# Loads, rounding steps and clamps moved in the start of a linear-attention and feed-forward kernel, and its last store split

## The chip, the cores and the metric

The kernel runs on one core of a Trainium2 chip. A core has a matrix engine (TensorE, PE in the profile, with its weight loads as PEld), a vector engine (VectorE, DVE), an engine for functions and copies (ScalarE, ACT), a general one (GpSimd, POOL) and a sequencer that issues transfers (SyncE, SP). Each takes its instructions in program order and waits on semaphores where an operand is not ready. TensorE writes to PSUM, the other engines compute between PSUM and the on-chip memory SBUF. The metric is the device time of one execution in microseconds (us); the lower the better.

## The reference, cut to what matters

```
# attention: B=4, H=8, S=768, D=48; q, k, v ~ 0.1 N(0,1), f_logit ~ 0.5 N(0,1) + 2
f = 1 / (1 + exp(-f_logit))
for t in range(S):
    state = f[:, :, t, :, None] * state + einsum('bhd,bhe->bhde', k[:, :, t], v[:, :, t])
    y[:, :, t] = einsum('bhd,bhde->bhe', q[:, :, t], state)
x = y as (3072 tokens, 384)
# feed-forward: w_in (384, 2048), w_out (2048, 384), both given as float64
h  = x @ w_in
sp = max(h, 0) + log1p(exp(-|h|))
out = (h * erf(sp)) @ w_out                     # (3072, 384), float32
```

## The kernel before, in words

The 3072 tokens are 24 chunks of 128 (six to a batch entry), taken as 12 blocks of two chunks. The recurrence is done chunk by chunk, and within a chunk in two halves of 64 tokens. Four functions make up a chunk g:

- `stage_d` (d): one prefix matmul of the block's log decays (L380) into PSUM, two Exp on ScalarE (L383, L386), eight small copies of the decay totals issued by SP (L391, from chunk 3 on), and on VectorE the products qd and kd (L395, L399).
- `stage_t` (t): eight transposes on TensorE (L411), copied out by ScalarE (L418 for q, L420 for k; k on VectorE, L422, from chunk 9 on). It also issues the second state update of the chunk before.
- `stage_s` (s): the outer products k v (L460) and the scores (L468) into one PSUM tile. For the first three chunks and from chunk 10 on VectorE masks the scores (L496); between these ScalarE copies them (L488) and GpSimd masks (L491). Then the first state update: four VectorE instructions, L438 and L439 twice.
- `stage_y` (y): 64 small matmuls (L525) that give the chunk's output, copied by ScalarE (L529) to `xT`, the input of the feed-forward part.

PSUM tiles of the tag "at" (prefix sums, both transposes, y) come from a ring of two, so y(g) waits for the copy L418 of the transposes issued two tiles ahead of it. The score tile has one buffer.

`prepare` makes the log decays of a block or of one chunk: a clamp on VectorE (L360), then Exp and Ln on ScalarE (L364, L365), with a load of the function table ahead (L347) when another was in use.

The feed-forward part of a block has four groups. A group is 12 slots of the main loop: `hidden` does four tiles of 128 hidden units with three matmuls each (a slot is one such matmul and appears as two L587 records), then ScalarE copies the group out (L594). `activate` does the nonlinearity of a group in a fixed train of calls to `act_step`: Exp (L157), two tanh (L160), two VectorE products (L165), three empty calls, one tanh (L559), one VectorE product (L561). A new group begins at the sixth call. Its Exp writes a buffer that the group two before has to free with L561. Groups of 1024 columns leave `hidden` through two PSUM tiles, so a group can begin only when the group two before has been copied out.

The weights arrive as float64 and are rounded to float32 on the chip. `load_piece` brings a piece of 768 KB into a spare place (SP, L292); `round_piece` rounds it in seven instructions: ScalarE's L311, then on VectorE L313, L317, L322, L326, L331 and L336. `weights_step` issues them one VectorE instruction at a time, six calls a piece; the call that issues L331 also issues L311 of the next piece. There are eight pieces of `w_in` and eight of `w_out`. A tile of the hidden layer may be issued only when its `w_in` piece is rounded (two tiles, six slots, to a piece), and the output matmuls need the `w_out` pieces.

The order of all instructions is written out by hand. A preamble does the first chunks (d(0), t(0), d(1), s(0), t(1), d(2), y(0), s(1), t(2), y(1)) with `weights_steps(2)` or `(4)` between them. Then the main loop makes twelve passes, `it` = 0 to 11. Pass 0 has 96 slots: the groups of blocks 0 and 1 in the order 0.0, 0.1, 1.0, 0.2, 1.1, 0.3, 1.2, 1.3. Pass 1 has the 48 slots of block 2. Pass 2 has the 48 slots of block 3 and then 32 of `project_first`, the output matmuls of block 0 (L670). Later passes do the output of one block by seven products in place of eight (`project`, L718) and the hidden layer of another; the last pass does the output of three blocks. After each slot the loop body, in this order, adds to `due` and issues one rounding step for each whole unit, issues a stage when the slot's number is next in the list `at`, issues clamp, Exp and Ln of a later block at fixed slots, and calls `act_step` at slots set by the pass (every sixth in pass 1, two in five in pass 2). So a rounding step in the program stands ahead of the stage and the activation step of the same slot on VectorE's queue.

In `project` the sums of the seven products are made on VectorE (L726) as they become complete, and `store` sends a block's 384 KB with one transfer on SP (L654).

Of the kernel before, what the change touches and what calls it, by code (L numbers as in the profile page):

```python
# [43 lines left out]
FP32 = mybir.dt.float32  # L44
# [26 lines left out]
P = 128  # L71
# [3 lines left out]
def kernel(  # L75
# [10 lines left out]
    nc = tc.nc  # L86
# [10 lines left out]
    CPB = 2  # L97
    TB = CPB * P
    n_blocks = B * S // TB
# [95 lines left out]
    DH = d_model // 2  # L195
# [147 lines left out]
    def use_exp_ln():  # L343
        if sets[0] == EXP_LN:
            return
        sets[0] = EXP_LN
        nc.scalar.add_instruction(  # L347
            mybir.InstLoadActFuncSet(
                act_func_set_id=EXP_LN, name=nc.get_next_instruction_name(),
                engine=mybir.EngineType.Activation, ins=[], outs=[],  # L350
            )
        )
# [3 lines left out]

    def prepare(blk, j0, j1):

        lt = lts[blk][:, j0:j1, :].rearrange("t j c -> t (j c)")
        nc.vector.tensor_scalar(  # L360
            out=lt, in0=lt, scalar1=LOGIT_MIN, scalar2=None, op0=ALU.max
        )
        use_exp_ln()
        nc.scalar.activation(out=lt, in_=lt, func=AF.Exp, scale=-1.0)  # L364
        nc.scalar.activation(out=lt, in_=lt, func=AF.Ln, bias=1.0)  # L365

    busy = []
# [284 lines left out]
    def store(blk):  # L652
# [4 lines left out]
        )  # L657

    def project_first(blk):

# [26 lines left out]
    def project(blk):  # L687
# [7 lines left out]
        }.items()}  # L695
        first = [1, 2, 5, 3]

        def pair(n):
# [38 lines left out]
        def fives():  # L737

            plus(o[:, 3:5, :], o[:, 4:5, :].broadcast_to((P, 2, DH)), pair(5))

        yield from products((2, 3), (5, 7))
        if end:

            fives()
        yield from products((2, 3), (3, 4))
        if not end:
            fives()
        plus(o[:, 1:3, :], o[:, 3:5, :], pair(3))
# [44 lines left out]
    with tc.manual_schedule():  # L793
# [7 lines left out]
        load_f(1)  # L801
        load(1, "qk")
        load_f(2)
        load_piece(0)
        load(1, "v")
        load(2)
        load_piece(1)
        load_piece(2)
# [47 lines left out]
        def weights_steps(n):  # L856
            for _ in range(n):
                weights_step()
# [6 lines left out]
        prepare(0, 1, 2)  # L865
        stage_t(0)
        load(3, "qk")
        load_piece(3)
# [44 lines left out]
        for it in range(n_blocks):  # L913
            gen, n = slots(it)
            if it == 0:
                todo = [(stage_s, 2), (stage_y, 2), (stage_d, 3), (stage_t, 3), (stage_s, 3), (stage_y, 3),
                        (stage_d, 4), (stage_t, 4), (stage_d, 5), (stage_s, 4), (stage_t, 5),
                        (stage_y, 4)] + stages(2)[4:]
                at = [1, 5, 6, 12, 16, 23, 34, 42, 48, 52, 60, 74, 76, 80, 88, 94]
            else:  # L920
                todo = stages(it + 2) if it + 2 < n_blocks else []
                at = [n * x // 48 for x in (2, 6, 11, 17, 25, 29, 34, 41)] if it == 1 else [int(3 + (n - 13) / max(1, len(todo)) * i) for i in range(len(todo))]
# [7 lines left out]
            for s, _ in enumerate(gen):  # L930
                due += (1 if s < 42 else 0.6 if s < 72 else 0.3) if it == 0 else 0.42 if it == 1 else 0.6
                while due >= 1:
# [4 lines left out]
                if at and s == at[0]:  # L937
# [3 lines left out]
                    if f in (stage_y, stage_y_s):  # L941
# [3 lines left out]
                        if g == 2:  # L945
                            load(5, "v")
                            load_piece(7)
                if it == 0 and s == 14:
                    prepare(2, 0, CPB)
                if it == 0 and s == 9:  # L950
                    load_f(6)
                    load_f(7)
                if s == n // 2 and it + 4 < n_blocks:
                    for j in range(CPB):
                        load_f((it + 4) * CPB + j)
                if it + 3 < n_blocks and s == prepare_at:
                    prepare(it + 3, 0, CPB)
                if it < 2:
# [242 lines left out]
```

## Time and profile before

| what | value |
| --- | --- |
| time, median of 7 runs | 618.9 us (618.78 to 619.81) |
| profiled execution | 619.97 us, its span 618.3 us |
| TensorE busy | 588.6 us (95%) |
| VectorE busy | 460.4 us (74%) |
| ScalarE busy | 382.3 us (62%) |
| pass 0 begins (first L587) | 28.33 us |
| pass 1, pass 2 begin | 105.92 us, 135.24 us |
| first output matmul (L670) | 164.4 us |
| last matmul ends | 611.1 us |

The span runs from the first to the last instruction; the time of an execution includes a little around it. "Busy" is the union of an engine's instructions. In a timeline row the first number is the start in us, the second the duration, then engine, line of the kernel, operation, what it writes and reads, shapes and count; what stands in brackets at its end is how long the engine stood idle before it and what ended the wait. The row PEclk gives the granted clock of TensorE in 40 equal slices, in tenths of full speed.

### The profile page before, as it was taken

What the parts mean: (1) busy time and instruction counts of PE and PEld (TensorE: products, weight loads), DVE (VectorE), ACT (ScalarE), POOL (GpSimd) and SP (SyncE); (2) the same over time, 40 slices, a digit from 0 to 9 for tenths busy, and PEclk for the clock granted to TensorE, in tenths of its full rate; (3) what the DMA queues carried; (4) which work ended last, traced back from release to release, by engine and by line L of the source; (5) the groups of instructions that cost most, each with busy time, mean ns of one, the idle gap of its engine ahead of it and who ended that gap; (6) DMA issues with size and microseconds to landing.
All of it is one profiled execution on the core that took longest, in us unless ns stands there. A gap on an engine that the chain in (4) does not pass through costs nothing.

```text
span 618.3 us, 13765 instructions
## 1 busy us (share of the span) xinstructions
PE 588.6 (95%) x5729; PEld 514.5 (83%) x5729; DVE 460.4 (74%) x784; ACT 382.3 (62%) x483; POOL 15.2 (2%) x33
## 2 busy tenths in 40 slices
PE   8778899999999999999999999999999999999995
PEld 7556687888655689989989989989989989989995
DVE  4998998697499597897796776896886785647451
ACT  5735357987875778775866675875766566366000
POOL 1000011010000000000000000000000000000000
PEclk9987899999999999999999999999999999999999
DMA  9996753350241223223223222132121000000000
GB/s 206 252 259 180 201 157 63 65 103 10 50 77 27 51 54 52 43 62 54 44 60 53 45 59 53 29 77 53 34 46 14 3 27 0 28 1 0 27 27 29
DMA packets 155587, 41.35 MB, mean 67 GB/s; under 512 B 147328, under 2 KB 150400, under 8 KB 155520
## 3 DMA queue, kind: packets, MB, share of 16 engines
q1 hardware_dynamic: 153440, 40.02, 29.7%
q8 instruction: 47, 0.77, 0.5%
q10 hardware_dynamic: 2080, 0.39, 0.3%
q14 instruction: 20, 0.16, 0.1%
HBM read 35.59 MB, written 4.72 MB: 65 GB/s over the span
## 4 chain that ended last, share of the span: by engine, by line
PE 75%; DVE 11%; ACT 7%; DMA 3%; issue 2%; SPq 1%; POOL 0%; ACTq 0%; DVEq 0%; POOLq 0%
PE hps L587 32%; PE ops L718 25%; PE ops L670 7%; PE y L525 3%; PE ps_t L411 3%; PE ps_d L380 2%; ACT x L160 2%; PE sc L460 1%; PE sc L468 1%; DMA Hg<-in_moe_w_in_dram 1%; DVE sv L439 1%; DVE sv L438 1%; DVE Hg L561 1%; DVE w_in_sb L336 1%; DVE w_in_sb L322 1%
## 5 line engine op out<-in xcount | busy, mean ns | idle before, releaser
L587 PE MATMUL hps<-xT,w_in_sb 128*128 128x256 f32 x1152 | 265.1, 386 | 5.1 <-DVE w_in_sb L336 2.8
L587 PEld LDWEIGHTS hps<-xT,w_in_sb 128*128 128x128 f32 x1152 | 218.8, 193 | 39.4 <-ACT xT L529 2.8
L165 DVE SCALAR_TENSOR_TENSOR e<-x,e 128x1024 f32<-128x1024 f32 x96 | 117.1, 1220 | 13.1 <-ACT x L160 12.6
L160 ACT ACTIVATE x<-Hg,serf_bias 128x1024 f32<-128x1024 f32 x88 | 97.5, 1141 | 0.2
L157 ACT ACTIVATE e<-Hg 128x1024 f32<-128x1024 f32 x44 | 46.5, 1058 | 61.7 <-DVE Hg L561 57.7
L718 PE MATMUL ops<-wT,Hg 128*128 128x192 f32 x320 | 78.9, 328 | 0.0
L561 DVE TENSOR_TENSOR Hg<-Hg,e 128x1024 f32<-128x1024 f32 x44 | 53.8, 1222 | 22.2 <-ACT e L559 21.9
L718 PE MATMUL ops<-wT,scratch 128*128 128x192 f32 x288 | 67.8, 326 | 0.9 <-DVE scratch L726 0.9
L718 PE MATMUL ops<-w_out_sb,Hg 128*128 128x192 f32 x320 | 65.1, 326 | 0.0
L594 ACT COPY Hg<-hps 128x1024 f32<-128x1024 f32 x44 | 44.4, 1009 | 32.8 <-PE hps L587 32.5
L718 PEld LDWEIGHTS ops<-wT,Hg 128*128 128x128 f32 x320 | 55.8, 190 | 1.9
L718 PEld LDWEIGHTS ops<-w_out_sb,Hg 128*128 128x128 f32 x320 | 54.6, 190 | 2.0
L559 ACT ACTIVATE e<-e 128x1024 f32<-128x1024 f32 x48 | 50.3, 1048 | 1.9 <-DVE e L165 1.8
L718 PEld LDWEIGHTS ops<-wT,scratch 128*128 128x128 f32 x288 | 50.3, 190 | 1.1 <-issue 1.1
L496 DVE TENSOR_TENSOR qA<-sc,tri 64x256 f32<-64x256 f32 x68 | 28.7, 422 | 24.5 <-PE sc L468 23.6
L726 DVE TENSOR_TENSOR scratch<-scratch,ops 128x384 f32<-128x384 f32 (+1 forms) x40 | 20.1, 503 | 31.8 <-ACT scratch L734 24.5
L525 PEld LDWEIGHTS y<-qA,sv 128*32 128x32 f32 x1536 | 24.7, 112 | 19.0 <-issue 11.4
L525 PE MATMUL y<-qA,sv 128*32 128x64 f32 x1536 | 29.6, 225 | 10.4 <-issue 4.5
L418 ACT COPY qA<-ps_t 64x512 f32<-64x512 f32 x48 | 27.7, 577 | 19.0 <-PE ps_t L411 17.1
L395 DVE TENSOR_TENSOR qd<-qn,dp 128x384 f32<-128x384 f32 x24 | 13.4, 557 | 33.1 <-ACT dp L383 32.7
L718 PE MATMUL ops<-w_out_sb,scratch 128*128 128x192 f32 x144 | 35.2, 326 | 0.0
L438 DVE TENSOR_TENSOR sv<-sc,sv 48x192 f32<-48x192 f32 x80 | 28.4, 355 | 8.3 <-ACT qA L488 6.9
(111 smaller groups left out, 649.0 us busy)
## 6 DMA issues: line engine op xcount, KB each, us to landing
lt<-in_f_logit_dram SPq DMA_DIRECT2D x24, 192.0 KB, 3.7
qn<-in_q_dram SPq DMA_DIRECT2D x24, 192.0 KB, 3.2
out_dram<-scratch SPq DMA_DIRECT2D x12, 384.0 KB, 2.6
kn<-in_k_dram SPq DMA_DIRECT2D x23, 192.0 KB, 3.5
vt<-in_v_dram SPq DMA_DIRECT2D x23, 192.0 KB, 3.6
sv<-in_v_dram SPq DMA_DIRECT2D x84, 48.0 KB, 2.9
w_out_sb<-in_moe_w_in_dram SPq DMA_DIRECT2D x4, 768.0 KB, 5.7
Hg<-in_moe_w_in_dram SPq DMA_DIRECT2D x4, 768.0 KB, 6.2
```

The costliest lines, as they stand in the source:

```text
L157: nc.scalar.activation(out=dst[:], in_=h, func=AF.Exp)
L160: nc.scalar.activation(out=dst[:], in_=h, func=AF.Tanh, bias=serf_bias[:, i : i + 1], scale=SERF_KAB[i][0])
L165: nc.vector.scalar_tensor_tensor(out=e[:], in0=x[:], scalar=SERF_KAB[i][2], in1=e[:], op0=ALU.add, op1=ALU.mult)
L438: nc.vector.tensor_tensor(out=new, in0=add, in1=old, op=ALU.add)
L496: nc.vector.tensor_tensor(out=qA[half(1 - r), r, :, half(c)], in0=sc[half(c), r], in1=tri1[half(c)].unsqueeze(1).broadcast_to((C, HP, C)), ...
L525: nc.tensor.matmul(y[M * i : M * (i + 1), kt, half(c)], lhsT=sv[:, r, c, a, o : o + M], rhs=qA[:, r, a, half(c)], start=(n == 0), stop=Tru ...
L559: nc.scalar.activation(out=e[:], in_=e[:], func=AF.Tanh, scale=SERF_C)
L561: nc.vector.tensor_tensor(out=h, in0=h, in1=e[:], op=ALU.mult)
L587: nc.tensor.matmul(hps[:, j, :], lhsT=w_in_sb[:, kt, ft * P : (ft + 1) * P], rhs=xTs[blk][:, kt, :], start=(kt == 0), stop=(kt == n_k - 1),)
L594: nc.scalar.copy(out=gr["h"], in_=hps[:])
L670: nc.tensor.matmul(ops[:, tt, 0:d_model], lhsT=gr["h"][:, j, tt * P : (tt + 1) * P], rhs=w_out_sb[:, ft, :], start=(ft == 0), stop=(ft == ...
L718: nc.tensor.matmul(place[n], lhsT=x[:, j, :], rhs=y, start=(gi == 0 and j == 0 and n in first), stop=(gi == n_g - 1 and j == 1), skip_grou ...
```

## The change: what it does

- SP's order of loads in the preamble: the first `w_in` piece goes ahead of the loads of chunk 1, and the second one and chunk 1's v ahead of the third f_logit chunk.
- Two of the rounding steps are issued after t(0), in addition to those that were there.
- The rate of rounding steps becomes 1 per slot up to slot 17, 0.46 up to slot 65 and 0.3 to the end of pass 0, then 0.55 in all later passes (before: 1 up to slot 41, 0.6 up to slot 71, 0.3, then 0.42 in pass 1 and 0.6 later).
- `prepare` is divided into `clamp` and `logs`. In the loop a clamp is issued six slots ahead of its Exp and Ln. For block 2 the clamp stands at slot 18 and Exp and Ln at slot 24 of pass 0 (before: both at slot 14).
- In pass 0 d(3) comes before y(2), at slot 5, and y(2) at slot 8; d(4) moves from slot 34 to 36 and t(4) from 42 to 43.
- In the last block product 4 gets a PSUM tile of its own, product 3 is finished first, and the block is stored as two tiles of 128 rows, the first on SP and the second on ScalarE's queue.

```diff
-    def prepare(blk, j0, j1):
-
+    def clamp(blk, j0, j1):
         lt = lts[blk][:, j0:j1, :].rearrange("t j c -> t (j c)")
         nc.vector.tensor_scalar(
             out=lt, in0=lt, scalar1=LOGIT_MIN, scalar2=None, op0=ALU.max
         )
+
+    def logs(blk, j0, j1):
+
+        lt = lts[blk][:, j0:j1, :].rearrange("t j c -> t (j c)")
         use_exp_ln()
         nc.scalar.activation(out=lt, in_=lt, func=AF.Exp, scale=-1.0)
         nc.scalar.activation(out=lt, in_=lt, func=AF.Ln, bias=1.0)
+
+    def prepare(*which):
+        clamp(*which)
+        logs(*which)
...
+    def store_tile(blk, t, queue):
+        r = blk * TB + t * P
+        queue.dma_start(
+            out=out[r : r + P, :],
+            in_=rows_sb[:, 2 * t : 2 * t + 2, :].rearrange("p two c -> p (two c)"),
+        )
...
         first = [1, 2, 5, 3]
+        if end:
+            place[4] = ps_at.tile([P, 512], FP32, name="ops4", tag="at")[:, 0:DH]
+            first.append(4)
...
             fives()
+            yield from products((2, 3), (3,))
+            plus(o[:, 1, :], o[:, 3, :], place[3])
+            store_tile(blk, 0, nc.sync)
+            plus(o[:, 3, :], o[:, 3, :], place[7])
+            yield from products((2, 3), (4,))
+            plus(o[:, 2, :], o[:, 4, :], place[4])
+            store_tile(blk, 1, nc.scalar)
+            return
         yield from products((2, 3), (3, 4))
-        if not end:
-            fives()
+        fives()
...
         load_f(1)
-        load(1, "qk")
+        load_piece(0)
+        load(1, "qkv")
+        load_piece(1)
         load_f(2)
-        load_piece(0)
-        load(1, "v")
         load(2)
-        load_piece(1)
         load_piece(2)
...
         stage_t(0)
+        weights_steps(2)
         load(3, "qk")
...
-                todo = [(stage_s, 2), (stage_y, 2), (stage_d, 3), (stage_t, 3), (stage_s, 3), (stage_y, 3),
+                todo = [(stage_s, 2), (stage_d, 3), (stage_y, 2), (stage_t, 3), (stage_s, 3), (stage_y, 3),
...
-                at = [1, 5, 6, 12, 16, 23, 34, 42, 48, 52, 60, 74, 76, 80, 88, 94]
+                at = [1, 5, 8, 12, 16, 23, 36, 43, 48, 52, 60, 74, 76, 80, 88, 94]
...
-                due += (1 if s < 42 else 0.6 if s < 72 else 0.3) if it == 0 else 0.42 if it == 1 else 0.6
+                due += (1 if s < 18 else 0.46 if s < 66 else 0.3) if it == 0 else 0.55
...
-                if it == 0 and s == 14:
-                    prepare(2, 0, CPB)
+                if it == 0 and s == 18:
+                    clamp(2, 0, CPB)
+                if it == 0 and s == 24:
+                    logs(2, 0, CPB)
...
+                if it + 3 < n_blocks and s == prepare_at - 6:
+                    clamp(it + 3, 0, CPB)
                 if it + 3 < n_blocks and s == prepare_at:
-                    prepare(it + 3, 0, CPB)
+                    logs(it + 3, 0, CPB)
```

## The prediction

> **What bounds the kernel now.** I read the page's engine shares first, then busy time by stretches, then the timeline around each wait of TensorE.
>
> ```profile
> span 618.3 us, 13765 instructions
> PE 588.6 (95%) x5729; PEld 514.5 (83%) x5729; DVE 460.4 (74%) x784; ACT 382.3 (62%) x483; POOL 15.2 (2%) x33
> PEclk9987899999999999999999999999999999999999
> ```
>
> TensorE is the bound on average, and its clock dips only in the first eighth. The stretches (TensorE, weight loads, VectorE, ScalarE, GpSimd busy; granted clock) cut the run at the passes of the main loop: pass 0 is 28.3 to 105.9, pass 1 to 135.2, the hidden half of pass 2 to 164.4.
>
> ```profile
> 28.30:77.00 48.70, 39.18 (x380) 30.87 (x381) 45.01 (x76) 19.82 (x31) 1.31 (x2) 0.83 0.81 209
> 77.00:105.90 28.90, 28.90 (x358) 23.79 (x356) 27.14 (x45) 16.86 (x29) 4.49 (x6) 1.00 0.47 116
> 105.90:135.20 29.30, 28.89 (x373) 24.30 (x373) 21.90 (x38) 26.78 (x38) 3.18 (x4) 1.00 0.42 73
> 135.20:164.40 29.20, 27.14 (x302) 22.25 (x301) 17.50 (x24) 23.46 (x29) 1.50 (x2) 1.00 0.29 52
> 189.10:611.10 422.00, 420.12 (x3828) 380.83 (x3826) 307.12 (x526) 257.83 (x295) 1.01 (x4) 1.00 0.19 37
> ```
>
> After 189 us TensorE hardly waits, so only the start, passes 0 to 2 and the tail can move. Up to 77 us VectorE is the bound (45.0 of 48.7); from 77 to 105.9 TensorE never waits although VectorE is 94% busy; in pass 1 ScalarE is 91% busy. The timeline says how the queues meet:
>
> ```profile
> 51.00 0.84 ACT L364 ACTIVATE lt<-lt 128x768 f32<-128x768 f32 x1 [2.65 <-DVE lt L360]
> ...
> 72.33 0.85 PE L411 MATMUL ps_t<-ident,qd 128*128 128x128 f32 x4 [3.08 <-DVE qd L395]
> ...
> 121.44 0.56 DVE L313 TENSOR_SCALAR w_out_sb<-w_out_sb 128x768 f32<-128x768 f32 x1 [2.57 <-ACT w_out_sb L311]
> ...
> 139.33 1.22 DVE L561 TENSOR_TENSOR wT<-wT,e 128x1024 f32<-128x1024 f32 x1
> ...
> 140.65 1.06 ACT L157 ACTIVATE e<-Hg 128x1024 f32<-128x1024 f32 x1 [1.97 <-DVE wT L561]
> ...
> 151.50 1.21 PE L525 MATMUL y<-qA,sv 128*32 128x64 f32 x64 [0.88 <-issue]
> ...
> 611.13 0.94 DVE L726 TENSOR_TENSOR scratch<-scratch,ops 128x384 f32<-128x384 f32 x2 [2.04 <-PE ops L718]
> ...
> 612.10 0.37 SPq L654 DMA_DIRECT2D out_dram<-scratch  x1
> ```
>
> The row at 72.33 is chunk 4's transposes waiting for its products behind rounding. The rows at 139 to 151 are a chain without slack: rounding ends at 137.35 on VectorE, L561 frees the buffer that ScalarE's next Exp (L157) wants, ScalarE then copies chunk 9's transposes (L418), which frees the PSUM that y(8) needs.
>
> **Unit costs.** A rounding step is one VectorE instruction but the first of a piece (a ScalarE L311, 0.9, goes with the fifth). Start to start from 75.03 to 79.67 (L313, L317, L322, L326, L331, L336): 0.58 + 0.60 + 0.99 + 0.60 + 1.00 + 0.87 = 4.64 a piece, 0.77 a step. A slot of the main loop (two matmul records) is 0.4325 at full clock. A state update (L438/L439, four) is 1.55, L395 with L399 1.05, a clamp 0.55, L165 and L561 1.2 each.
>
> **Steps done, before and after, counted from the rates.** End of the preamble 10 and 12; slot 41 of pass 0: 52 and 41; end of pass 0: 77 and 61; end of pass 1: 96 (all) and 87; the other nine at slots 0, 2, 4, 6, 8, 10, 11, 13, 15 of pass 2. So 16 steps, 12.4 us of VectorE, leave pass 0 for passes 1 and 2.
>
> **Preamble.** Piece 0 moves past q, k of chunk 1, pieces 0 and 1 past f_logit of chunk 2 on SP's queue. By the landing records chunk 1's logits land at 7.41, then q 0.91, k 0.86, f 0.81, piece 2.56, v 0.94, second piece 1.94 later. In the new order piece 0 lands near 10.0 (12.55), q and k at 10.9 and 11.7 (not wanted before 12.6), v at 12.7 (13.49), piece 1 near 15 (18.77), chunk 2's logits at 15.4 to 16.1 (9.99); I take 15.8. L311 of piece 0 now stands on ScalarE between kT (ends 12.19) and chunk 1's Exp, so L313 and L317 run at 13.1 to 14.3, L395/L399 to 15.3 (13.65), the clamp of chunk 2 at 15.8 (13.57). Laying VectorE on from there, the twelfth step ends at 35.2; in the trace the twelfth ends at 34.76. Slot 0 waits for xT(1) instead of piece 0: 29.9 against 28.33. The start gives nothing, it costs VectorE 0.4.
>
> **Pass 0.** From 35.2 VectorE has, up to L399 of chunk 4, 26 steps (20.1), chunk 2's masks and total (1.95), four state updates (6.2), two pairs L395/L399 (2.1), one clamp (0.55): 66.1. The same sum for before, 33 steps from 34.76 with its idle 1.85, gives 72.9; the trace has 72.65. Slot 24 stays near 57.8 (58.02): y(3) needs a state update with 17 steps ahead of it, ending at 56.0; that Exp and Ln now come after y(3) removes only ScalarE's 2.65, which VectorE hides. From 57.8 TensorE needs 20 slots (8.65) and the prefix matmul (0.66): 67.1, and the products are there. Transposes 0.87: slot 44 at 68.0 (74.68), slot 48 at 69.7 (77.07). Gain 7.4 at full clock. If the clock halves after the wait for y(3), as it does in the trace from 55.5 to 62.35, it is 5.0. From slot 48 on TensorE is the bound in both. I take 6.1; ends 4 and 7.6.
>
> **Moved stages.** y(2) goes from slot 5 to 8, so three slots run ahead of its masks, for which TensorE waited 0.8, 1.0 and 0.5 us (35.5 to 38.3); VectorE is what comes next there, so the gain is already in 66.1. On SP the values for chunk 4 and piece 7 follow y(2) and go out some 1.4 us later; piece 7 landed at 48.88 and its first step is the 43rd, after 66. Chunk 3's prefix matmul comes ahead of y(2), so SP's eight small copies from it (43.73 to 49.37) go out earlier; the update that reads them is bound by VectorE. The later moves (34 to 36, 42 to 43) cost the slots counted above.
>
> **Passes 1 and 2, on the clock of before.** ScalarE from L488 of chunk 6 (ends 112.4): L311 0.9, table and tanh 2.4, L594 1.0, L418 and L420 1.8, table, Exp and Ln 3.0, table and tanh 2.4, xT 0.5, L311 0.9: 125.3. The 12th step of the pass (L313) waits for that last L311, and VectorE, idle since 121.3, starts at 125.4 (121.44). Queued behind it are L395/L399 of chunk 8, ending 129.9 (126.6), so TensorE, at 127.5 in the trace, waits some 2 us for them. Then without a gap: 15 steps 11.6, two L165 2.4, one L395 pair 1.05, two updates 3.1, ending pass 1 at 143.5 (137.35 in the trace); two steps 1.6, L165, the L395 pair, L561: 148.5, where the trace has 140.55. ScalarE's L157 waits for it. Then L165, seven steps 5.4, an update, L165, a clamp, L561: 159.6 (149.12). L157 and L418 follow, so y(8) starts near 161.8 instead of 151.50. Queued behind that L157 are L594 and Exp/Ln, so slot 36 of pass 2 is late too; it waited 0.76 already, and I take 9.6 in all. Upper end: all 16 steps, 12.4. Lower end: pass 1's seven fit its 7.4 us of VectorE idle, and of pass 2's nine (6.9) 3.5 fall in the one idle stretch before 145.21: 3.4. I stay near the upper end, because instructions start in program order, and the idle lies ahead of waits that also stop the steps.
>
> **Clock after that wait.** TensorE would stand some 8 us before y(8); a wait of 5.2 us before slot 24 cost half clock for 11 records, 2.3 us. ScalarE is the bound just behind y(8), so most hides: 0.8 (0 to 2.3).
>
> [...]
>
> **Clamps.** Those of blocks 3 and up move six slots up a queue that has room (307 of 422 busy): nothing; without that room 0.55 each.
>
> **Tail.** Last matmul ends 611.10, two sums to 612.08, store issued 612.10 to 612.48, landed 616.73. New: one 192-wide sum (0.35) to 611.5, then a store of half the size on ScalarE's queue, the other half already under way. The issue is 0.6 earlier; the three last full stores took 3.80, 2.44 and 4.63 to land, so half a store saves 0 to 1. I take 0.9 (0.4 to 1.6). The added PSUM tile is free long before.
>
> **Sum.** -6.1 + 9.6 + 0.8 - 0.9 = +3.4 on the span of 618.3. The profiled execution took 619.97, 1.1 over the median of 618.9; I set the difference on the median: 622.3.
>
> **Rivals.** *Idle time swallows the late steps:* passes 1 and 2 cost 3.4, no clock loss: -6.1 + 3.4 - 0.9 = -3.6, 615.3. For it: VectorE is only 75% busy in pass 1, 60% behind. Against: the chain above has no slack. It decides once passes 1 and 2 cost less than 7.0. *The two cancel:* they cost about 7, 619. *Worse:* the clock halves after y(3) (gain 4) and all 16 steps show (12.4, clock 1.5, tail 0.4): +9.5, 628; ScalarE at 91% in pass 1 speaks for it. *The rates do nothing:* chunk 4's transposes wait for something else, such as the Exp and Ln now at slot 24; those have 3 us of cover, so I give that no separate chance.
>
> **Numbers.** Forecast case 0.58, worse 0.10, cancel 0.07, swallowed 0.25. The measurement can tell 0.2% (1.2 us): slower 0.68, same 0.07, faster 0.25. Range 615.5 to 627, leaving out half of each outer case; the forecast alone 620 to 626.
>
> **What would show it.** L411 of chunk 4 without its 3 us wait, and slot 48 some 5 to 7 us earlier; L336 rows in pass 2; L313 waiting about 4 us on L311 in pass 1; L157 waiting 4 to 8 us for L561; y(8) after a wait of 5 us or more; the final store's landing some 1 us after its half-size sum comes sooner. I am wrong if L561 in pass 2 keeps its place against slot 0, or if slot 48 hardly moves.

## The result, and the profile after

The changed kernel takes 621.12 us (median of 18 runs, 619.52 to 623.41), the kernel before on the same chip 619.21 us (median of 42, 618.29 to 620.26). The ratio is 1.0033, with a 95% interval of 1.0025 to 1.0040: slower by some 2.0 us. The forecast was 622.3.

The profiled execution of the changed kernel took 620.06 us, its span is 618.4 us. The profiled one of before took 619.97 us and is thus 0.8 above its median, while this one is 1.1 below its own. So the two traces differ by 0.1 us only, and where the time went has to be read stretch by stretch, not from the spans.

The page after: span, busy time by engine, granted clock in 40 slices.

```profile
span 618.4 us, 13759 instructions
PE 585.4 (95%) x5729; PEld 511.8 (83%) x5729; DVE 460.9 (75%) x785; ACT 382.9 (62%) x483; POOL 14.6 (2%) x33
PEclk9899999998899999999999999999999999999999
```

The dips of the clock in the third to fifth slices are gone; there is one in the second (14.7 to 21.6 us) and one in the tenth and eleventh (151.3 to 158.1 us). The same stretches as before, after the change (stretch, length, busy time of TensorE, weight loads, VectorE, ScalarE and GpSimd with their instructions, granted clock, DMA share, GB/s); the last row is the rest of the run from the fourth pass on, moved by 2.1 us:

```profile
28.30:77.00 48.70, 39.86 (x501) 31.88 (x502) 44.62 (x78) 23.23 (x39) 3.27 (x4) 1.00 0.82 212
77.00:105.90 28.90, 28.90 (x360) 24.06 (x359) 20.20 (x36) 18.13 (x31) 3.26 (x6) 1.00 0.61 147
105.90:135.20 29.30, 27.29 (x303) 22.60 (x302) 24.86 (x39) 25.93 (x35) 1.78 (x2) 1.00 0.40 69
135.20:164.40 29.20, 21.10 (x207) 17.34 (x206) 22.41 (x31) 18.52 (x23) 1.52 (x2) 0.88 0.16 28
...
191.20:613.20 422.00, 420.11 (x3828) 380.83 (x3826) 307.73 (x527) 257.93 (x295) 1.01 (x4) 1.00 0.19 37
```

From 28.3 to 77 us TensorE does 501 matmul records, where it did 380. VectorE is busy 20.2 us from 77 to 105.9 (27.1 before) and 22.4 from 135.2 to 164.4 (17.5 before): the late rounding. In that last stretch TensorE has fallen from 27.1 to 21.1 us and from 302 records to 207. From the fourth pass on nothing has changed (420.1 of 422).

The timeline after. The first row is VectorE's clamp of the third chunk's logits, the second TensorE's transposes of chunk 4, then the rows that answer to the chain in passes 1 and 2, then the tail:

```profile
15.90 0.36 DVE L359 TENSOR_SCALAR lt<-lt 128x384 f32<-128x384 f32 x1 [1.52 <-DMA lt<-in_f_logit_dram]
...
66.95 0.60 PE L418 MATMUL ps_t<-ident,qd 128*128 128x128 f32 x4
...
117.47 0.56 DVE L313 TENSOR_SCALAR w_out_sb<-w_out_sb 128x768 f32<-128x768 f32 x1 [3.61 <-ACT w_out_sb L311]
...
139.18 1.22 DVE L568 TENSOR_TENSOR wT<-wT,e 128x1024 f32<-128x1024 f32 x1
...
140.50 1.06 ACT L157 ACTIVATE e<-Hg 128x1024 f32<-128x1024 f32 x1 [6.91 <-DVE wT L568]
...
149.99 1.22 DVE L568 TENSOR_TENSOR wT<-wT,e 128x1024 f32<-128x1024 f32 x1
...
151.24 1.06 ACT L157 ACTIVATE e<-wT 128x1024 f32<-128x1024 f32 x1 [4.21 <-DVE wT L568]
...
152.31 1.17 ACT L425 COPY qA<-ps_t 64x512 f32<-64x512 f32 x2
...
153.58 2.05 PE L532 MATMUL y<-qA,sv 128*32 128x64 f32 x64 [7.61 <-issue]
...
612.31 0.34 SPq L668 DMA_DIRECT2D out_dram<-scratch  x1
...
613.61 0.37 ACTq L668 DMA_DIRECT2D out_dram<-scratch  x1
```

The transposes of chunk 4 have no wait in brackets any more. The price stands at 140.50 and 151.24: ScalarE's Exp (L157) waits 6.91 and 4.21 us for VectorE's product (L568, L561 before) to let go of a buffer, the copy of the transposes (L425, L418 before) stands behind the second of these, and y(8) starts 0.1 us after that copy, after a wait of 7.61 us.

Where the profiled time went, before and after:

| place | before | after | change to that point |
| --- | --- | --- | --- |
| slot 0 | 28.33 | 29.73 | +1.4 |
| slot 24 of pass 0 | 58.02 | 57.56 | -0.5 |
| slot 48 of pass 0 | 77.07 | 69.55 | -7.5 |
| pass 1 begins | 105.92 | 98.28 | -7.6 |
| first output matmul | 164.38 | 166.92 | +2.5 |
| pass 11 begins | 555.22 | 557.31 | +2.1 |
| last matmul's end to the end of the span | 7.17 | 5.17 | +0.1 |

### The profile page after: what moved, and what is told of

The parts are those of the page before. It is cut to its first block, busy times and chain, and to the rows that moved or that the text cites. A ratio compares the mean times of both kernels' runs of the same rounds, so it can differ in the third digit from the quotient of the medians.

```text
span 618.4 us, 13759 instructions
## 1 busy us (share of the span) xinstructions
PE 585.4 (95%) x5729; PEld 511.8 (83%) x5729; DVE 460.9 (75%) x785; ACT 382.9 (62%) x483; POOL 14.6 (2%) x33
## 3 DMA queue, kind: packets, MB, share of 16 engines
q1 hardware_dynamic: 153312, 39.82, 29.4%
## 4 chain that ended last, share of the span: by engine, by line
PE 77%; DVE 11%; issue 4%; ACT 4%; SPq 3%; DMA 1%; DVEq 0%; ACTq 0%
PE hps L594 34%; PE ops L735 25%; PE ops L684 7%; PE y L532 3%; PE ps_t L418 2%; PE ps_d L387 2%; PE sc L475 1%; PE sc L467 1%; SPq L234 1%; DVE sv L445 1%; DVE sv L446 1%; ACT x L160 1%; DMA vt<-in_v_dram 1%; DVE w_out_sb L331 1%; DVE w_in_sb L322 1%
## 5 line engine op out<-in xcount | busy, mean ns | idle before, releaser
L594 PE MATMUL hps<-xT,w_in_sb 128*128 128x256 f32 x1152 | 261.8, 383 | 5.3 <-DVE w_in_sb L336 2.7
L594 PEld LDWEIGHTS hps<-xT,w_in_sb 128*128 128x128 f32 x1152 | 216.3, 191 | 38.8 <-DVE w_in_sb L336 3.9
L165 DVE SCALAR_TENSOR_TENSOR e<-x,e 128x1024 f32<-128x1024 f32 x96 | 117.6, 1225 | 13.2 <-ACT x L160 12.6
L160 ACT ACTIVATE x<-Hg,serf_bias 128x1024 f32<-128x1024 f32 x88 | 97.5, 1140 | 0.2
L157 ACT ACTIVATE e<-Hg 128x1024 f32<-128x1024 f32 x44 | 46.5, 1058 | 66.6 <-DVE Hg L568 57.6
L568 DVE TENSOR_TENSOR Hg<-Hg,e 128x1024 f32<-128x1024 f32 x44 | 53.8, 1222 | 22.6 <-ACT e L566 22.3
L425 ACT COPY qA<-ps_t 64x512 f32<-64x512 f32 x48 | 27.7, 578 | 17.0 <-PE ps_t L418 16.5
```

The costliest lines, as they stand in the source:

```text
L157: nc.scalar.activation(out=dst[:], in_=h, func=AF.Exp)
L160: nc.scalar.activation(out=dst[:], in_=h, func=AF.Tanh, bias=serf_bias[:, i : i + 1], scale=SERF_KAB[i][0])
L165: nc.vector.scalar_tensor_tensor(out=e[:], in0=x[:], scalar=SERF_KAB[i][2], in1=e[:], op0=ALU.add, op1=ALU.mult)
L568: nc.vector.tensor_tensor(out=h, in0=h, in1=e[:], op=ALU.mult)
L594: nc.tensor.matmul(hps[:, j, :], lhsT=w_in_sb[:, kt, ft * P : (ft + 1) * P], rhs=xTs[blk][:, kt, :], start=(kt == 0), stop=(kt == n_k - 1),)
```

## The experiments

Times are medians with lowest and highest; each ratio is to the kernel before on the same chip, with its 95% interval. The places are from the one profiled execution of each kernel.

| kernel | time, us | runs | ratio | slot 0 | slot 48 | pass 1 begins | wait ahead of y(8) | first output matmul |
| --- | --- | --- | --- | --- | --- | --- | --- | --- |
| changed kernel | 621.12 (619.52 to 623.41) | 18 | 1.0033 (1.0025 to 1.0040) | 29.73 | 69.55 | 98.28 | 7.61 | 166.92 |
| its split store alone | 618.04 (617.01 to 619.32) | 8 | 0.9982 (0.9970 to 0.9993) | 27.44 | 76.15 | 104.98 | 0.81 | 163.40 |
| its rates alone | 623.76 (622.97 to 625.97) | 4 | 1.0082 (1.0063 to 1.0100) | 28.29 | 69.51 | 102.21 | 6.76 | 168.62 |
| old rates | 620.64 (619.94 to 623.12) | 10 | 1.0021 (1.0009 to 1.0032) | 29.48 | 78.39 | 107.12 | 1.28 | 166.84 |
| old rates, old start | 617.76 (617.13 to 619.11) | 12 | 0.9983 (0.9974 to 0.9992) | 28.32 | 76.26 | 104.99 | 1.31 | 163.90 |
| old start | 619.02 (616.78 to 620.71) | 12 | 0.9987 (0.9975 to 0.9998) | 28.01 | 67.38 | 101.02 | 7.21 | 166.75 |
| new order of loads, no early steps | 620.73 (619.53 to 622.15) | 12 | 1.0024 (1.0013 to 1.0036) | 30.50 | 70.10 | 101.46 | 7.23 | 167.24 |
| old order of loads, early steps | 621.67 (620.33 to 622.88) | 7 | 1.0035 (1.0019 to 1.0051) | 29.37 | 70.87 | 99.59 | 7.61 | 168.67 |
| late rates | 615.29 (613.47 to 616.81) | 6 | 0.9939 (0.9919 to 0.9959) | 29.54 | 69.34 | 98.07 | 1.29 | 160.18 |
| even rates | 615.67 (614.01 to 617.34) | 6 | 0.9940 (0.9921 to 0.9959) | 29.58 | 71.09 | 99.82 | 3.84 | 162.11 |
| a buffer of its own | 617.12 (614.73 to 619.58) | 8 | 0.9962 (0.9943 to 0.9980) | 29.89 | 72.50 | 101.23 | 0.74 | 166.60 |
| even rates and buffer | 609.23 (607.46 to 611.38) | 5 | 0.9844 (0.9823 to 0.9864) | 29.39 | 70.88 | 99.61 | none | 156.21 |
| even rates, buffer, old start | 608.29 (606.15 to 608.39) | 5 | 0.9810 (0.9796 to 0.9825) | 27.60 | 66.51 | 95.38 | 0.30 | 153.16 |

### The changed kernel with the old rates

```diff
-due += (1 if s < 18 else 0.46 if s < 66 else 0.3) if it == 0 else 0.55
+due += (1 if s < 42 else 0.6 if s < 72 else 0.3) if it == 0 else 0.42 if it == 1 else 0.6
```

> The changed kernel with the rounding rates of before (all else as changed). Theory (the rates both give the gain up to slot 48 of pass 0 and cost the wait in pass 2): 11 more steps, 8.5 us, stand ahead of chunk 4's products again, so slot 48 is back near 77 us or a little behind it, and the wait before y(8) in pass 2 shrinks from 7.61 to about 1 us; passes 1 and 2 take the 58.5 us up to the first output matmul that they took before; the tail keeps its 2 us. Time near 618 us (616.5 to 619.5). Rival (the loads, the early steps and the clamps give the gain in pass 0): slot 48 stays near 70 us and the time is near 610 us.

The wait ahead of y(8) goes (1.28 us in place of 7.61) and the one ahead of chunk 4's transposes comes back: 7.16 us. That is what the theory expected of the two waits; the time of 620.64 is 1.1 above the theory's range, and far from the rival's. So the rates alone do not make the changed kernel slower by 2 us: with the old ones it is slower too (1.0021, interval 1.0009 to 1.0032). Something else in the change costs time.

### The new rates alone, in the kernel before

The same line, the other way round, in the kernel before.

> The kernel before with the new rounding rates and nothing else. Theory (rates alone carry both gain and loss): chunk 4's products have 25 steps in place of 33 ahead of them, slot 48 near 70 to 73 us, some half clock left; 59 steps are done at the end of pass 0, so eleven fall into pass 2 and y(8) waits 8 to 10 us there; no gain at the tail. Time 621.1 + 2.0 for the tail, + up to 2 for the two steps more and the clock: 622 to 626 us. Rival (the other parts carry the gain of pass 0): slot 48 near 77 us and the time 627 to 630 us.

Time and slot 48 came as the theory expected; the wait ahead of y(8), 6.76 us, is shorter than its 8 to 10. Slot 48 stands at 69.51 against 69.55 of the changed kernel: the rates alone carry the whole gain of pass 0, 7.6 us. And the rates alone make the wait ahead of y(8). But pass 1 begins at 102.21, not at 98.28, because of this row of TensorE in pass 0. It waits 2.02 us, and its 18 records take 5.84 us, where 18 take 4.05 in the trace of before (at 146.57, clock 1.00); from these two some 3.6 us at half rate are an estimate:

```profile
82.17 5.84 PE L587 MATMUL hps<-xT,w_in_sb 128*128 128x256 f32 x18 [2.02 <-DVE w_in_sb L336]
```

With ten steps done in the preamble in place of twelve, the slower rates bring a piece of `w_in` too late: the two other traces with ten steps and these rates have this wait too (2.96 and 2.37 us, in the runs on the start below), the changed kernel does not. In medians the rates alone cost 4.3 us (623.76 against 619.43 for the kernel before on that chip).

### The split store alone, in the kernel before

The diff is the part of the change in `project` and `store_tile`.

> The kernel before with the last block's split store and nothing else. Theory: the stretch from the last matmul to the end falls from 7.2 to 5.2 us and nothing else moves: 619.2 - 2.0 = 617.2 us (616.7 to 618). Rival (what the tail of the changed kernel gained came from elsewhere): the time stays within 0.5 us of 619.2.

The store pays, but less than expected: 1.1 us in place of 2.0 (ratio 0.9982, interval 0.9970 to 0.9993), a time just past the upper end of the theory's range. In the profile the stretch from the last matmul to the end falls from 7.17 to 5.12 us.

### The late rates

```diff
-due += (1 if s < 18 else 0.46 if s < 66 else 0.3) if it == 0 else 0.55
+due += (1 if s < 18 else 0.46 if s < 44 else 0.69) if it == 0 else 0.42 if it == 1 else 0.6
```

> The changed kernel with its rates of pass 0 up to slot 43 (1, then 0.46), but 0.69 a slot from slot 44 to 95 and the old 0.42 in pass 1, so that 77 steps are done at the end of pass 0 and all 96 at the end of pass 1, as before. Theory (the loss is only that VectorE stands idle in the second half of pass 0, where it was busy 20.2 of 28.9 us, and the 16 steps come back on the chain of passes 1 and 2): slot 48 stays at 69.6 us, TensorE does not wait from there to the end of pass 0, y(8) waits about 1 us, and passes 1 and 2 take 58.5 us up to the first output matmul in place of 68.6. Time 621.1 - 10.2, near 611 us (609.5 to 613). Rival (the slot where the steps are issued matters little, passes 1 and 2 are late because pass 0 ends 7.6 us earlier, for instance with transfers not landed): passes 1 and 2 keep most of their 68.6 us, time 617 to 621 us.

The place of the rounding is what counts, as the theory had it: slot 48 keeps its gain, y(8) has its short wait again, and the kernel is faster than both. Its median is 2.3 us above the theory's upper end; the profiled execution (613.80) is 0.8 above it, and TensorE shows what cost time there:

```profile
107.30 0.63 PE L418 MATMUL ps_t<-ident,qd 128*128 128x128 f32 x4 [1.95 <-DVE qd L402]
```

VectorE's rounding from the end of pass 0 is still queued when pass 1 wants the products of chunk 7. Behind this wait of 1.95 us the clock fell: in the mean of 98 to 130 us it was 0.95, an estimated 3.2 us at half rate. The kernel's six times stand in two groups, 613.5 to 613.9 and 616.7 to 616.8; I did not find out what parts them.

### Rates between the two

```diff
+due += (1 if s < 18 else 0.46 if s < 44 else 0.6) if it == 0 else 0.48 if it == 1 else 0.6
```

> The changed kernel with the rounding rates 1 (first 18 slots), 0.46 (to slot 44), 0.6 (to 96) in pass 0 and 0.48 in pass 1. 73 steps are then due by the end of pass 0 instead of 60 in the changed kernel (77 with the late rates), and 96 instead of 86 by the end of pass 1. Theory (VectorE has room behind slot 44 and what is rounded there need not be rounded in passes 1 and 2; the late rates lost 2 to 4 us because their last steps were still queued when pass 1 asked VectorE for qd): slot 48 stays at 69.3 to 69.7, the wait of TensorE ahead of the seventh transpose, 1.95 us with the late rates, falls below 0.8, the wait ahead of y(8) stays at 1 to 2.5, and the time is 611 to 613.5. Rival (the rounding costs the same wherever it lies once it is out of the first 48 slots, and the late rates were only a better clock): 617 or more, with the wait ahead of y(8) at 4 or more.

A miss. The wait ahead of chunk 7's transposes is gone, but y(8) waits 3.84 us and the matmuls behind that are slow (14 records from 150.38 take 4.89 us, where 14 take 3.29 in the trace of before, at 152.64 and clock 1.00), so that the gain at one place is lost at the other and the time is that of the late rates. Slot 48 missed its place as well (71.09, expected 69.3 to 69.7), although the order of the instructions up to slot 43 is still that of the late rates, which have slot 48 at 69.34; what held it up was not shown. Neither theory nor rival had the number.

### A buffer of its own for the third group's Exp

```diff
-        e = epool.tile([P, FG * TB], FP32, name="e", tag="e")
+        own = gr["own"]
+        if own:
+            e = wT[:, 2:4, FG * TB :]
+            h = h.rearrange("p (a b) -> p a b", a=2)
+        else:
+            e = epool.tile([P, FG * TB], FP32, name="e", tag="e")
...
-        gr = {"h": h_group(blk, gi), "done": False, "sums": None}
+        gr = {"h": h_group(blk, gi), "done": False, "sums": None, "own": (blk, gi) == (1, 0)}
```

> The changed kernel, where the third group to be activated (block 1, group 0) gets a buffer e of its own in a free part of wT, so that its Exp need not wait until the first group's product L568 has let go of a buffer; rounding and everything else stay. Theory (the rounding steps hold up the products of VectorE, Exp in ScalarE's queue waits for these products' buffer, and the copy qA that y(8) needs is queued behind that Exp): the 6.91 us that the third group's Exp waits and the 4.21 of the fourth's go or move to the x buffers (free at 137.5 and 141.5 in the profile), y(8)'s wait falls from 7.61 to 0.5 to 3.4, and the time to 614 to 617.5. Rival (VectorE's backlog itself holds y(8), by whatever path): the wait stays above 5 and the time at 620 to 622.

This is the test of the prediction's chain. The theory holds: y(8) waits 0.74 us in place of 7.61, with all the rounding where the change put it, and the time falls by 0.71% (ratio 0.9962, interval 0.9943 to 0.9980, against 1.0033). ScalarE's queue, and TensorE's two waits:

```profile
136.39 1.07 ACT L157 ACTIVATE wT<-Hg 128x1024 f32<-128x1024 f32 x1
140.42 1.16 ACT L160 ACTIVATE x<-Hg,serf_bias 128x1024 f32<-128x1024 f32 x1 [2.96 <-DVE e L165]
...
147.61 1.17 ACT L425 COPY qA<-ps_t 64x512 f32<-64x512 f32 x2
152.41 1.15 ACT L160 ACTIVATE x<-wT,serf_bias 128x1024 f32<-128x1024 f32 x1 [3.62 <-DVE wT L165]
```

```profile
148.88 0.91 PE L532 MATMUL y<-qA,sv 128*32 128x64 f32 x36 [0.74 <-issue]
...
157.68 0.70 PE L601 MATMUL hps<-xT,w_in_sb 128*128 128x256 f32 x2 [3.58 <-ACT Hg L608]
```

The Exp at 136.39 waits for nothing. What is late next is the tanh (L160), which waits for the x buffers that VectorE's L165 frees, 2.96 and 3.62 us. The second of these lies behind the copy that y(8) needs and ahead of the copy-out (L608) that frees TensorE's PSUM: so 3.58 us of the wait move from y(8) to there. VectorE's backlog is still there; the buffer only took away its shortest way to TensorE.

### The even rates and the buffer together

> The changed kernel with the even rates (1, 0.46, 0.6; 0.48 in pass 1) and the third group's own buffer e together. Theory (both take away the same wait ahead of y(8), so that together they bring little more than the even rates alone): 0 to 1.5 us under the even rates alone, 610 to 613. Rival (the two waits are separate): 3 us or more under the even rates alone.

The rival was right: the two together take 6.4 us less than the even rates alone. The 3.84 us ahead of y(8) in these rates were that same buffer, and with it go the slow matmuls that followed. TensorE in the stretches of passes 1 and 2, at a granted clock of 1.00:

```profile
105.90:135.20 29.30, 28.05 (x312) 23.76 (x311) 26.14 (x41) 26.53 (x36) 4.55 (x4) 1.00 0.41 70
135.20:164.40 29.20, 29.20 (x308) 22.91 (x307) 21.57 (x31) 27.25 (x35) 2.99 (x4) 1.00 0.25 42
```

It is busy for the whole of 135.2 to 164.4 us, where the changed kernel had 21.10, although VectorE is nearly as busy there (21.57 against 22.41); by these rates the rounding ends at 134.4 us, in the changed kernel at 149.6. From the start of pass 1 to the first output matmul it takes 56.6 us, against 68.6 in the changed kernel and 58.5 before.

### The start

Two runs put the old start back: once with the old rates, once with the new. A third does so in the fastest version.

```diff
-        load_piece(0)
-        load(1, "qkv")
-        load_piece(1)
+        load(1, "qk")
         load_f(2)
+        load_piece(0)
+        load(1, "v")
         load(2)
+        load_piece(1)
         load_piece(2)
...
         stage_t(0)
-        weights_steps(2)
```

> The changed kernel with the old rounding rates, the old order of the loads on SyncE's queue in the preamble and without the two early rounding steps: what is left of the change is the clamps ahead of the logarithms, the moved stages and the last store in two parts. Theory (the new start costs its 1.4 us at slot 0 and is worth nothing without the new rates): 618 to 620, 1 to 2 us under the changed kernel with old rates (620.64) and at most 1 us over the split store alone (618.04), with slot 0 back at 28.3. Rival (the new start is harmless, the moved clamps and stages cost): 620 to 622.

> The changed kernel, new rates and all, but with the old order of the loads in the preamble and without the two early rounding steps (slot 0 then starts near 28.3 again, 1.4 us earlier). Theory (the new start costs 2 to 3 us by itself, 617.76 against 620.64 with old rates, but the slower rates need it: with two steps fewer done, the last w_in pieces are rounded too late in pass 0, where the before-kernel with the new rates alone waited 2.02 us at 82.17, and two more steps fall into passes 1 and 2): 622 to 624.5, with a wait of TensorE for L336 between slots 50 and 66 of pass 0. Rival (the new start costs the same with the new rates): 617.5 to 619.5, and no such wait.

> The fastest version so far (even rates and the third group's own buffer e, 609.23) with the old start in the same way. Theory: it loses the 1.4 us of slot 0 again in pass 0 by the wait for L336, and the two steps that move on have room: 609 to 611.5. Rival (the new start costs 2 to 3 us also here): 606 to 607.5.

In all three pairs the new start costs time. With the old rates it is 0.38% (0.9983 to 1.0021), with the new ones 0.46% (0.9987 to 1.0033), in the fastest version 0.34% (0.9844 to 0.9810, five runs each, and the two intervals just touch): 2.1 to 2.8 us. With the old rates the theory was right that the start costs time, and the time is 0.2 below its range. The theory expected the second and the third run to lose by the old start; the wait it named was there (2.96 us at 80.97, and 18 records behind it in 5.84 us, as with the rates alone), but the rival was right on the second time, and the third, 608.29, lies between the two; there the even rates, which round more behind slot 44, left no such wait. The clamp of the third chunk and that wait, with the old start and the new rates:

```profile
13.25 0.35 DVE L359 TENSOR_SCALAR lt<-lt 128x384 f32<-128x384 f32 x1
```

```profile
80.97 3.36 PE L594 MATMUL hps<-xT,w_in_sb 128*128 128x256 f32 x9 [2.96 <-DVE w_in_sb L336]
```

Beside the split store alone (0.9982), the run with old rates and old start (0.9983) also says that the clamps and the moved stages are worth nothing there. Slot 42 comes 4.6 us earlier in its profile (63.57 against 68.16; how much of it the clock gave was not shown, the mean clocks of the two executions are 0.988 and 0.986), and then TensorE waits 7.02 us for chunk 4's products instead of 2.63:

```profile
71.62 1.09 PE L418 MATMUL ps_t<-ident,qd 128*128 128x128 f32 x4 [7.02 <-DVE qd L402]
```

With the new rates, which take that wait away, they pay: the rates alone give 1.0082 (1.0063 to 1.0100), the change with the old start 0.9987, and the store is only 0.18% of this. In the two traces slot 24 comes 2.1 us earlier by them (57.51 and 55.40) and slot 48 keeps this (69.51 and 67.38).

Two more runs take the start apart: the new order of loads without the two early steps, and the old order with them.

> The changed kernel without the two early rounding steps, with its new order of the loads. The new start as a whole costs 2.1 us (621.12 against 619.02 with the old start). Theory A (the order of the loads costs it: the third chunk's logits land at 15.88 in place of 9.99, VectorE's clamp waits for them 1.52 us and stands at 15.9 in place of 13.3, and all that follows up to slot 0 is late by it): 620.5 to 622.5, the clamp still at 15.9 and slot 0 at 29 or later. Theory B (the two steps, 1.5 us of VectorE ahead of what slot 0 needs, cost it): 618 to 619.8 and slot 0 near 28.3.

> The changed kernel with its two early rounding steps, but the old order of the loads. Theory A (the order costs it): the logits of the third chunk are there at 10, but ScalarE's first rounding instruction waits for piece 0, landing at 12.5, ahead of the second chunk's Exp, so some 1 us of the 2.1 comes back in another place: 619.5 to 621. Theory B (the two steps): as the changed kernel, 620.5 to 622.5, with slot 0 at 29.5 or later.

Each half alone costs about what both cost together (1.0024 and 1.0035 against 1.0033, and 0.9987 with neither). Theory A is right on the first run, theory B on the second, so neither was the whole. VectorE's clamp in the first of the two runs, and in the second ScalarE's first rounding instruction and the clamp:

```profile
15.76 0.36 DVE L359 TENSOR_SCALAR lt<-lt 128x384 f32<-128x384 f32 x1 [2.10 <-DMA lt<-in_f_logit_dram]
```

```profile
12.63 0.90 ACT L311 ACTIVATE w_in_sb<-w_out_sb 128x768 f32<-128x768 f32 x1 [0.80 <-DMA w_out_sb<-in_moe_w_in_dram]
13.43 0.48 ACT L390 ACTIVATE dp<-ps_d 128x384 f32<-128x384 f32 x1
...
15.57 0.35 DVE L359 TENSOR_SCALAR lt<-lt 128x384 f32<-128x384 f32 x1
```

In both the clamp that stood at 13.25 stands at 15.6 to 15.8, by two ways. With the new order the logits come late. With the old order piece 0 comes late for the early step: ScalarE's L311 waits for it until 12.63, the Exp of chunk 1 (L390) stands behind that, VectorE's products behind these, and the clamp behind the products. Both also leave slot 0 at 29.4 to 30.5 against 28.0.

With the old rates the traces show where the time goes, since both lie within 0.4 us of their medians (620.65 with the new start, 617.36 with the old). The clamp stands at 15.66 against 13.58, slot 0 at 29.48 against 28.32, slot 48 at 78.39 against 76.26, the first output matmul at 166.84 against 163.90. VectorE's products for chunk 4, for which TensorE waits some 7 us in both, come 2.4 us later, 1.5 us of it by two more rounding steps (L336, L313) that stand ahead of them; first the old start, then the new one:

```profile
70.92 0.55 DVE L402 TENSOR_TENSOR qd<-qn,dp 128x384 f32<-128x384 f32 x1
```

```profile
71.96 0.96 DVE L336 TENSOR_TENSOR w_in_sb<-Hg,w_in_sb 128x768 f32<-128x768 f32 x1
72.84 0.55 DVE L313 TENSOR_SCALAR w_out_sb<-w_out_sb 128x768 f32<-128x768 f32 x1
73.31 0.55 DVE L402 TENSOR_TENSOR qd<-qn,dp 128x384 f32<-128x384 f32 x1
```

With the new rates this stays open. In the profiled executions the early steps of the changed kernel are paid back: with the old start TensorE waits 2.96 us later in pass 0, and the two spans end 0.3 us apart. The 2.1 us show in the medians. The profiled execution with the old start (620.46) lies 1.4 above its median and that of the changed kernel 1.1 below its own, so these two traces do not say where in an average execution the difference lies.

## Why the prediction was right, and where it was not

**Direction and mechanism.** The mechanism was right, the direction partly by luck: with the old start the same change comes out at 0.9987. Rounding that leaves pass 0 makes room there and comes out in passes 1 and 2 through the chain L568, L157, copy, y(8). The run with a buffer of its own shows this chain as the cause of the wait, not only as rows that follow each other. The sign "L561 in pass 2 keeps its place against slot 0" was loosely put. Against the first slot of pass 2 this product moved from 4.1 to 9.3 us behind it; against the first slot of pass 0 it kept its place (111.0 and 109.5), because pass 0 had gained what the rounding then took.

**The gain of pass 0.** The mechanism was right; 6.1 was taken, 7.5 measured at slot 48 of the profiled execution. The steps of its working came out: the twelfth step ends at 35.04 (35.2), slot 24 is at 57.56 (57.8), slot 44 at 67.82 (68.0), slot 48 at 69.55 (69.7). I had these at full clock and then took off 1.3 for a clock that might halve after y(3). In this execution it did not: the granted clock was 1.00 from 28.3 to 77 us. In the trace of the even rates with the buffer, with the same start and the same rates up to slot 43, it was 0.96 there, an estimated 3.9 us at half rate, and slot 48 stands at 70.88: a gain of 6.2. With the even rates alone and the buffer alone it stands at 71.09 and 72.50: gains of 6.0 and 4.6. So 7.5 is the gain at full clock, and the runs do not refute the 6.1. The "wait of 5.2 us before slot 24", by which I sized the clock, is in the trace three waits of 1.70, 0.41 and 0.57 us with the matmuls of y(3) between them.

**Passes 1 and 2.** Taken 9.6 and 0.8 for the clock, measured 10.2 together: from the start of pass 1 to the first output matmul 68.64 us, before 58.46. L313 waits 3.61 us for L311 (some 4 expected), L157 6.91 and 4.21 (4 to 8), y(8) 7.61 (5 or more). Only chunk 8's transposes waited less, 0.31 us in place of 2. The clock was half from 151.3 to 158.1 us; y(8) starts at 153.58, so 4.5 us of matmuls ran at half rate and 2.3 us were lost, the upper end of my 0 to 2.3. It is inside the 10.2.

On the clock, the traces have half rate behind waits of very different length. In the trace of before it was granted from 72.6 to 76.0 us, behind the wait of 3.08 us at 72.33, and from 55.5 to 62.3, behind those of 1.70 and 0.41 us in y(3). Behind waits of 2.02 us (rates alone) and 2.96 us (old start) 18 records took 5.84 us in place of 4.05, and the 7.61 us ahead of y(8) in the changed kernel went with 6.8 us of half clock. A wait of 1.81 us in y(3), at 55.57, went with none in the changed kernel.

**The tail.** Taken 0.9, measured 2.0 in the profile and 1.1 in the time of the store alone. My working had the issue 0.6 earlier, which the last row of before (611.10 to 612.10) and of after (613.19 to 613.61) give as 0.58, and half a store saving 0 to 1. The rest is the store: the two halves landed 1.90 and 2.26 us after their issue, the full one 4.63. Of these 2.4 us, 1.0 did not reach the end of the span, which comes 2.5 us after the last landing in place of 1.5. The 2.0 is one draw: full stores of the same size took 2.44 to 4.63 us within the trace of before; in the trace of the rates alone, with one full last store, the stretch from the last matmul to the end is 6.15, and the twelve traces with the split store have 5.0 to 6.2 there. So the 1.1 is the better number, and the term was near.

**The step that failed: "The start gives nothing, it costs VectorE 0.4."** It costs 2.1 to 2.8 us. Each number in that step was near: clamp at 15.8 (15.90), slot 0 at 29.9 (29.73), slot 24 near 57.8. But I compared slot 24 with that of before, and found it unchanged. The moved stages and clamps alone would have brought it to some 55, as the runs with the old start have it (55.05 with the old rates, 55.40 with the new), and the late start took this back. Two parts of opposite sign at one place looked like two parts worth nothing. The runs give the change as these parts, by differences of the ratios: store -0.18%, clamps and moved stages +0.01%, start +0.38%, rates +0.12%, together +0.33%. I had the rates as the loss, -6.1 + 9.6 + 0.8 = +4.3 us; in the changed kernel they cost 0.7 us, and with the old start 0.2 (0.9983 to 0.9987), both within the intervals. These shares hold for this order only. In the kernel before, the same rates cost 4.3 us in medians, what I had for them; there the clamps and moved stages, which I put at nothing, take most of it back (1.0082 to 0.9987, with the store in it).

**The sum.** +3.4 predicted, +2.0 measured. By the terms of the profile it is -7.6 + 10.2 - 0.5 (given back between the first output matmul and pass 11) - 2.0 = +0.1; the rest, 1.9, is how the two profiled executions stand to their medians. So the total stood nearer to the median than its parts to the runs, and that is luck: I had the whole loss in the rates and nothing for the start, the clamps and the moved stages, and of these the start costs time where the clamps and moved stages give some back.

**The rivals.** *Idle time swallows the late steps* needed passes 1 and 2 to cost less than 7.0; they cost 10.2. With the buffer of its own the same rates cost 6.9 there (65.37 us from the start of pass 1 to the first output matmul, against 58.46), and the time came out below that of before, as the rival's own condition says: what kept the idle time from swallowing the steps was that one buffer as much as the steps. *The two cancel* needed a cost near 7 and a time of 619; the cost was 10.2, the time 2.1 above. *Worse* had its clock loss in pass 0, which did not come in the profiled execution (clock 1.00 from 28.3 to 105.9 us).

## A version faster than both

The even rates, the third group's buffer and the old start, with the clamps, the moved stages and the split store of the change, take 608.29 us, ratio 0.9810 (0.9796 to 0.9825): 1.9% faster than the kernel before and 2.2% faster than the changed one. Its page:

```profile
span 604.8 us, 13765 instructions
PE 581.0 (96%) x5729; PEld 509.3 (84%) x5729; DVE 462.6 (76%) x785; ACT 382.5 (63%) x483; POOL 16.6 (3%) x33
```

VectorE and ScalarE are as busy as ever (460.9 and 382.9 us in the changed kernel). The gain is time in which TensorE no longer waits or runs at half clock (mean clock 0.995, in the changed kernel 0.987), and 1.8 us behind the last matmul (5.33 against 7.17).

## What to carry to other kernels

Work moved into another engine's idle time is free only if nothing that stands behind it in a queue holds a buffer that somebody waits for; follow the moved work to the first buffer it holds back, and price that, because one more buffer there may turn the loss into a gain. A change of several parts is to be costed part by part against the kernel with the other parts in it: two parts of opposite sign at one place look like nothing, and here the part that seemed harmless made the whole slower. Where the effect is less than the spread between executions, a profiled execution is one draw, and it has to be placed against its own median before its span is compared.

## What the runs showed of the hardware

Ahead of the last matmul the half-clock stretches of TensorE were 3.4 or 6.8 us long in the two traces of before (28.2 to 31.6, 38.4 to 41.9, 55.5 to 62.3 and 72.6 to 76.0) and of the changed kernel (14.7 to 21.6 and 151.3 to 158.1). The one at 14.7 followed a wait of 0.80 us, at 13.97. Kernels with the same start, load order and rates up to slot 43 differ in the clock there: the changed kernel had 0.88 from 0 to 28.3 us and 1.00 from there to 77, the late rates 0.99 from 0 to 30 and 0.92 from 30 to 70, the even rates with the buffer 0.96 from 28.3 to 77. Runs of the changed kernel spread from 619.5 to 623.4 us at mean clocks of 0.976 to 0.994, more than those of before (618.3 to 620.3); the mean clock does not order them, the two slowest had 0.986. The two half-size stores on two queues had both landed 3.6 us after the first one's issue, although the second was issued 1.3 us later; one store of the whole took 4.63 us at the end of the trace of before, and 2.44 to 3.81 in the blocks ahead of it.
